# The end of the first batch: four weight chunks, two masks and two column means in new places

## The chip, the cores and the metric

The kernel runs on one core of a Trainium2 chip. The core has five engines that run side by side: TensorE (PE, matrix products), VectorE (DVE), ScalarE (ACT), GpSimd (POOL) and SyncE (SP, which here only issues DMAs). Each takes its own instructions strictly in the order in which the program lists them, and waits where an operand is not ready. The metric is the device time of one execution in microseconds; lower is better.

## The reference

Eight batches of eight heads, 576 positions, 64 channels a head. Attention keeps the 32 largest scores of each row; what comes out is mixed by a two-dimensional Fourier transform whose real part is added to it, normalised, and put through a two-layer network.

```python
scores = scale * np.matmul(q, k.transpose(0, 1, 3, 2))
kth = np.partition(scores, -top_k, axis=-1)[..., -top_k:-top_k + 1]
scores = np.where(scores >= kth, scores, -1000000000.0)
attn = np.exp(scores - scores.max(-1)); attn = attn / (attn.sum(-1) + 1e-09)
x = matmul(attn, v)                       # -> (8, 576, 512)
mixed = np.real(np.fft.fft(np.fft.fft(x, axis=1), axis=2))
u = x + mixed
un = (u - u.mean(-1)) / np.sqrt(u.var(-1) + 1e-06)
out = u + np.maximum(un @ w_ch1, 0.0) @ w_ch2      # 512 -> 2048 -> 512
```

The weights arrive as 64-bit floating point numbers, which the kernel itself turns into 32-bit ones.

## The kernel before

**Attention tiles.** Two heads make a pair, four pairs a batch. A pair has nine tiles of 128 rows of scores; 36 tiles are a batch, 288 the whole. For tile i, PE computes scores (`scores`, L355), ACT copies them to the tile S, and DVE finds the 32 largest of each row in four rounds: `top_ops` (L428) gives an L446 that finds eight maxima and an L448 that strikes them out, seven operations a tile. `bounds` (L451, POOL) prepares two numbers a row, called nt. `mask` (L466) is an ACT operation (L469) and a POOL subtraction (L472), `expo` (L476) the exponential on ACT (L480). In the first batch `transposes` (L532) turns the result by PE and copies it by ACT; in most later ones `plane` (L487, two ACT copies L493) and a transposing DMA do so. `attend` (L576) multiplies by v on PE, `attended` and `to_tokens` bring the result back to rows and normalise it on DVE (L612, L630, L637).

**Weights.** `weight_steps` (L191) converts 32 chunks of 128 x 512: 16 of w1 and 16 of w2. A chunk is loaded by SP into one of five slots of a tile with the tag hT, the same memory in which the hidden activations are kept later. It takes three ACT operations (L209, L225, L228), one DVE shift (L217) and two POOL joins (L236, L238). One chunk is converted beside each of 32 of the first 34 tiles. `centre` (L1433) then makes the columns of w1 zero-mean: PE computes the means of 512 columns in four products (cm, L1437), ACT copies them (L1451), POOL subtracts them from the weights (L1446).

**The end of a batch.** `fold_pair` (L689) adds and subtracts mirrored rows for a pair's 128 channels; POOL does three pairs, and in the first and last batch DVE does the last pair and everything else (`fold_ops`, L751). `fold_tails` (L741) does the 64 rows left over on POOL. `dft_tokens_both` (L780) is the transform along the sequence on PE (yp, L809), whose results ACT copies out (L834 to L847), and `dft_channels` (L849) that along the channels (mp, L860 and L864). `add_at_once` (L877, L880) adds it to x on DVE; `stats` and `rsqrt` follow on DVE (the last is the tile gi) and POOL (L928 to L933). `channels_first` (L935) turns the rows by PE (tpu) and copies them by ACT (unT, L951), and the hidden products (hp, L1055; hT, L1059) begin.

**What sets the order.** The program is written out step by step, one attention tile a step, in the loop at the end of the kernel. A table `plan` holds further work: `at(step, where, fn)` puts a function at a place of a step, and `run(i, where)` calls those due. In step i the loop calls, in this order, the plane copies of tile i-2, the place "convert" (ACT), expo of tile i-1, a list `fixed` of PE work (with the places "pe1", "pe2" and "pe") between which MLP units are strewn, the top-k of tiles i and i+1 (with "shift" among it), `bounds(i)`, in the first batch `mask(i)`, then what has been put off to the end (`late_now`) and the places "dve", "stats", "pool", "pool2" and "load". The order in which these calls are made is each engine's order. The parts around the change:

```python
start_of = [0] + [34 * n // len(wcs) for n in range(1, len(wcs))]
...
at(
    start_of[n1] + 2 + 8 * c if early else PER_BATCH - 4 + 2 * c, "pe1",
    lambda c=c, early=early: centre(c, early), 3.5,
)
...
at((end - 2 if first else end) + hp, "pool2", lambda b=b, hp=hp: fold_pair(b, nc.gpsimd, hp))
```

The first batch ends with tile 35; its fold, in step 37, stands at the place "dve", behind all top-k operations of that step. The scores of tiles 41 and 42, in step 38, stand ahead of the second half of the means and of the transform.

Of the kernel before, what the change touches and what calls it, by code (L numbers as in the profile page):

```python
# [86 lines left out]
def kernel(  # L87
# [1272 lines left out]
    nc.vector.memset(cc[:, 0:1], -1.0)  # L1360

    warm = small.tile([P, 1], F32, name="warm", tag="rd", bufs=6)
    kn0 = batp.tile([P, NC, 2, D], F32, name="kn0", tag="y")
# [55 lines left out]
    nc.sync.dma_start(out=out_list, in_=rows_d.ap())  # L1419
    start_of = [0] + [34 * n // len(wcs) for n in range(1, len(wcs))]  # L1420
    for n, s0 in enumerate(start_of):
# [11 lines left out]
    def centre(c, early):  # L1433
# [18 lines left out]

        if early:
            at(now[0] + 1, "convert", copy)
        else:
            copy()
        for dt in range(NDT):
# [5 lines left out]
    for c in range(DF // DM):  # L1463

        early = c < DF // DM // 2
        at(
            start_of[n1] + 2 + 8 * c if early else PER_BATCH - 4 + 2 * c, "pe1",
            lambda c=c, early=early: centre(c, early), 3.5,
        )
# [13 lines left out]
    for b in range(B):  # L1483
# [4 lines left out]
        for hp in range(NPB - 1):  # L1488
            at((end - 2 if first else end) + hp, "pool2", lambda b=b, hp=hp: fold_pair(b, nc.gpsimd, hp))
        quick = first or last  # L1490
# [98 lines left out]
    while i < N + 5 or plan or queue or sums:  # L1589
# [20 lines left out]
        last_scores = []  # L1610
        if PER_BATCH < j < N and j % PER_PAIR == 0 and by_dma(j):
            fixed.append(lambda: 0.0)
# [27 lines left out]
        n_tr = len(fixed)  # L1640
        if done is not None:
            fixed.append(lambda: transposes(done))
# [16 lines left out]
        turn(i - 3)  # L1659
        if by_dma(i - 1):  # L1660
            mask(i - 1)
        plane(i - 2, 0)
        plane(i - 2, 1)
        run(i, "convert")
        if short:
            expo(i - 1)
        for n, fn in enumerate(fixed):
            cost += fn()
            if n == n_mask:
# [5 lines left out]
                out_next.clear()  # L1675
            if n == min(n_tr, len(fixed) - 1) and PER_BATCH <= i - 1 < N:
                expo(i - 1)
# [26 lines left out]
        first, second = top_ops(i, (2, 3)), top_ops(i + 1, (0, 1))  # L1704
        for n in range(max(len(first), len(second))):
            for ops in (second, first):
                if n < len(ops):
                    ops[n]()
                if ops is first and n == len(first) - 1:
                    run(i, "shift")  # L1710
# [9 lines left out]
        if i < PER_BATCH:  # L1720
            mask(i, lambda: run(i, "join"))
        for fn in late_now:
            fn()
# [44 lines left out]
```

## Time and profile before

| | us |
|---|---|
| median of 3 runs | 1776.76 |
| lowest, highest | 1775.06, 1779.67 |
| profiled execution, its own time | 1780.27 |
| its span, from first to last instruction | 1778.5 |
| PE busy | 1632.1 (92%) |
| DVE busy | 1552.5 (87%) |
| ACT busy | 1278.8 (72%) |
| POOL busy | 906.6 (51%) |

The rows of the profile give a line, an engine, an operation, and `out<-in` by the names of the tiles, with buffer numbers left out. L217 is line 217 of the kernel. "Idle before" is how long the engine had stood still ahead of an instruction, with what ended the wait. Neighbouring instructions on DVE and ACT overlap a little in the trace, so that the step from one start to the next is somewhat less than a duration. The first batch's attention fills the first 225 us, its fold and transform lie between 225 and 250 us.

### The profile page before, as it was taken

What the parts mean: (1) busy time and instruction counts of PE and PEld (TensorE: products, weight loads), DVE (VectorE), ACT (ScalarE), POOL (GpSimd) and SP (SyncE); (2) the same over time, 40 slices, a digit from 0 to 9 for tenths busy, and PEclk for the clock granted to TensorE, in tenths of its full rate; (3) what the DMA queues carried; (4) which work ended last, traced back from release to release, by engine and by line L of the source; (5) the groups of instructions that cost most, each with busy time, mean ns of one, the idle gap of its engine ahead of it and who ended that gap; (6) DMA issues with size and microseconds to landing.
All of it is one profiled execution on the core that took longest, in us unless ns stands there. A gap on an engine that the chain in (4) does not pass through costs nothing.

```text
span 1778.5 us, 26295 instructions
## 1 busy us (share of the span) xinstructions
PE 1632.1 (92%) x7830; PEld 1040.9 (59%) x7830; DVE 1552.5 (87%) x3319; ACT 1278.8 (72%) x3136; POOL 906.6 (51%) x1268
## 2 busy tenths in 40 slices
PE   5666689999898989999999999999999999999998
PEld 3444455464455755566555755576566755577777
DVE  7999989999999999998999999999999999863121
ACT  6888759887787878876888778877978787653200
POOL 4768846655634565354544665356535564333000
PEclk7778799999999999999999999999999999999999
DMA  5333126651457855586557856595558655643151
GB/s 156 115 102 117 32 81 163 185 152 50 119 145 196 222 131 135 136 233 161 135 136 200 212 133 140 152 240 145 152 132 222 182 135 128 172 114 101 36 180 60
DMA packets 492926, 255.28 MB, mean 144 GB/s; under 512 B 364528, under 2 KB 483056, under 8 KB 492784
## 3 DMA queue, kind: packets, MB, share of 16 engines
q1 hardware_dynamic: 489008, 243.80, 52.5%
q0 software_dynamic: 2816, 9.44, 1.6%
q8 instruction: 63, 1.03, 0.2%
q14 instruction: 79, 0.65, 0.1%
q10 hardware_dynamic: 960, 0.36, 0.1%
HBM read 99.79 MB, written 84.74 MB: 104 GB/s over the span
## 4 chain that ended last, share of the span: by engine, by line
PE 48%; DVE 16%; ACT 16%; POOL 14%; issue 5%; DMA 2%; POOLq 0%; SPq 0%; DVEq 0%; ACTq 0%
PE hp L1055 18%; DVE m L446 7%; DVE wk L448 6%; PE o L585 6%; PE cw L1254 5%; POOL wk L472 5%; PE cv L1254 4%; PE sp L422 4%; ACT wk L469 3%; POOL fold L696 3%; PE cp L1120 2%; ACT wk L493 2%; PE cp L1082 2%; ACT S L425 2%; PE sp_t L392 1%
## 5 line engine op out<-in xcount | busy, mean ns | idle before, releaser
L472 POOL TENSOR_TENSOR wk<-S,wk 128x576 f32<-128x576 f32 x288 | 407.6, 1415 | 418.1 <-ACT wk L469 417.2
L446 DVE MAX8 m<-wk 128x8 f32<-128x576 f32 x864 | 617.4, 741 | 0.1
L1055 PE MATMUL hp<-unT,w 128*128 128x256 f32 (+1 forms) x2048 | 529.6, 409 | 6.8 <-ACT hT L1059 6.0
L1055 PEld LDWEIGHTS hp<-unT,w 128*128 128x128 f32 x2048 | 378.0, 191 | 112.0 <-ACT hT L1059 11.4
L448 DVE MATCH_REPLACE8 wk<-m,wk 128x576 f32<-128x576 f32 x576 | 424.8, 737 | 0.0
L469 ACT ACTIVATE wk<-S,nt 128x576 f32<-128x576 f32 x288 | 224.3, 779 | 96.8 <-POOL nt L455 96.3
L493 ACT COPY wk<-S 128x576 uint16<-128x576 uint16 x468 | 290.2, 673 | 0.0
L446 DVE MAX8 m<-S 128x8 f32<-128x576 f32 x288 | 214.5, 745 | 11.6 <-ACT S L396 11.6
L480 ACT ACTIVATE S<-wk,nt 128x576 f32<-128x576 f32 x234 | 185.1, 791 | 46.7 <-POOL wk L472 45.4
L448 DVE MATCH_REPLACE8 wk<-m,S 128x576 f32<-128x576 f32 x288 | 212.5, 738 | 0.0
L1082 PE MATMUL cp<-w,hT 128*128 128x512 f32 x448 | 206.0, 598 | 0.0
L1059 ACT ACTIVATE hT<-hp 128x320 f32<-128x320 f32 (+1 forms) x256 | 104.1, 411 | 140.7 <-PE hp L1055 139.7
L585 PE MATMUL o<-PT,v 128*64 128x256 f32 (+3 forms) x1440 | 196.1, 417 | 5.6 <-DVE wk L448 2.1
L422 PE MATMUL sp<-kT,qT 64*128 64x512 f32 (+1 forms) x528 | 160.1, 668 | 6.7 <-ACT S L414 3.6
L585 PEld LDWEIGHTS o<-PT,v 128*64 128x64 f32 x1440 | 113.2, 154 | 84.1 <-issue 24.8
L425 ACT COPY S<-sp 128x512 f32<-128x512 f32 (+1 forms) x264 | 141.7, 589 | 26.2 <-PE sp L422 25.2
L455 POOL TENSOR_TENSOR nt<-m,cc 128x2 f32<-128x2 f32 x288 | 58.7, 204 | 166.9 <-DVE m L446 160.4
L1254 PE MATMUL cw<-w,hT 128*128 128x256 f32 x512 | 119.7, 383 | 9.1 <-ACT ct L1225 6.2
L1082 PEld LDWEIGHTS cp<-w,hT 128*128 128x128 f32 x448 | 81.3, 193 | 75.1 <-issue 74.7
L392 PEld LDWEIGHTS sp_t<-kt,qT 128*128 128x128 f32 x320 | 51.7, 195 | 111.4 <-issue 73.3
L1254 PEld LDWEIGHTS cw<-w,hT 128*128 128x128 f32 x512 | 94.5, 190 | 27.3 <-ACT ct L1225 8.4
L1254 PE MATMUL cv<-w,hT 128*128 128x256 f32 x432 | 100.4, 383 | 6.6 <-DMA w<-w_parts 2.8
(155 smaller groups left out, 2036.3 us busy)
## 6 DMA issues: line engine op xcount, KB each, us to landing
planes<-wk SPq DMA_DIRECT2D x208, 288.0 KB, 2.7
w<-w_parts SPq DMA_DIRECT2D x94, 512.0 KB, 4.7
space<-in_moe_w_ch_dram SPq DMA_DIRECT2D x32, 512.0 KB, 3.6
nat<-in_q_dram SPq DMA_DIRECT2D x128, 64.0 KB, 2.3
v<-in_v_dram SPq DMA_DIRECT2D x32, 256.0 KB, 3.4
nat<-in_k_dram SPq DMA_DIRECT2D x62, 128.0 KB, 2.8
planes<-wk SPq DMA_DIRECT2D x52, 144.0 KB, 2.7
w_parts<-w_t POOLq DMA_DIRECT2D x8, 512.0 KB, 4.0
```

The lines of the kernel that those rows point to most:

```text
L422: nc.tensor.matmul(sp[r], lhsT=qT[hd, q_cols], rhs=kT[hd, :], start=True, stop=True)
L425: nc.scalar.copy(out=s_t[r, keys], in_=sp[r])
L446: ops.append(lambda src=src, m8=m8: nc.vector.max(out=m8, in_=src))
L448: ops.append(lambda src=src, m8=m8: nc.vector.match_replace(w, m8, src, NEG))
L469: nc.scalar.activation(out=w, in_=Ssb[i], func=AF.Relu, scale=-FAR, bias=Nt[i][:, 1:2])
L472: nc.gpsimd.tensor_tensor(out=w, in0=Ssb[i], in1=w, op=ALU.subtract)
L480: nc.scalar.activation(out=Ssb[i] if by_dma(i) else w, in_=w, func=AF.Exp, bias=Nt.pop(i)[:, 0:1], accum_out=den_t[pair % 3][:, c:c + 1],)
L493: nc.scalar.copy(out=words[:, half, :], in_=src[:, half, :])
L585: nc.tensor.matmul(o[D * e:D * (e + 1), c0:c1], lhsT=vv[:, e, c, :], rhs=pt[:, NF if c == NF else (NF + 1) * e + c, c0:c1], start=(c == 0) ...
L1055: nc.tensor.matmul(hp[:, 0:w], lhsT=w1[:, dt, P * it:P * (it + 1)], rhs=unT[:, dt, 0:w], start=(dt == 0), stop=(dt == NDT - 1),)
L1082: nc.tensor.matmul(cp, lhsT=hT[:, it, P * n:P * (n + 1)], rhs=w2[:, it, :], start=(it == 0), stop=(it == NIT - 1),)
L1254: nc.tensor.matmul(dst, lhsT=h()[a][:, kc, :], rhs=rhs_of(kc), start=start and kc == 0, stop=kc == NK - 1, skip_group_check=True,)
```

## The change

Names by the new code: step 37 is `FOLD_STEP`.

- Of the 32 weight chunks, the last four (the last 512 rows of w2) are no longer converted beside a tile. Their twelve ACT operations stand in step 37 ahead of that step's other ACT work, their four shifts on DVE directly behind the fold, their eight joins on POOL behind it, the last four in step 38. The other 28 are spread over the same 34 steps.
- In step 37 the fold is moved into the top-k list: three operations of tiles 37 and 38 that stood ahead of it now stand behind.
- POOL gets a copy of one column of the fold's last result to an otherwise unused tile, `behind`. Since POOL works in order, what follows there starts when the fold has ended: the subtraction of mask(36), the joins.
- mask(36), moved from the start of step 38; expo(36), plane(36), mask(37), expo(37) and the scores of tiles 41 and 42, which stood ahead of the transform, come behind it.
- The means of w1's first half are computed in steps 21 and 26 instead of 19 and 27, those of the second half in steps 32 and 34 instead of 36 and 38, all of them behind the scores of the step, and their copies by ACT a step later each.
- POOL's folds of the first three pairs stand in steps 31, 33 and 34 instead of 33, 34 and 35.
- In step 35 the transposition of tile 34 goes behind mask(35).

The rest of the program's order is as before.

```diff
+    behind = const.tile([P, 1], F32, name="behind", tag="behind")
...
-    start_of = [0] + [34 * n // len(wcs) for n in range(1, len(wcs))]
+    FOLD_STEP = PER_BATCH + 1
+    LATE = 4
+    n_soon = len(wcs) - LATE
+    start_of = [0] + [34 * n // n_soon for n in range(1, n_soon)]
+    for n in range(n_soon, len(wcs)):
+        at(FOLD_STEP, "convert", lambda n=n: scale_high(n))
+        at(FOLD_STEP, "convert", lambda n=n: rest(n))
+        at(FOLD_STEP, "shift_late", lambda n=n: shift(n))
+        late = n - n_soon
+        for part in range(2):
+            at(
+                FOLD_STEP + late // 2, "join_late" if late == 0 else "pool",
+                lambda n=n, part=part: join(n, part),
+            )
...
-        if early:
-            at(now[0] + 1, "convert", copy)
-        else:
-            copy()
+        at(now[0] + 1, "convert", copy)
...
-            start_of[n1] + 2 + 8 * c if early else PER_BATCH - 4 + 2 * c, "pe1",
+            start_of[n1] + 2 + 5 * c if early else PER_BATCH - 8 + 2 * c, "pe",
...
-            at((end - 2 if first else end) + hp, "pool2", lambda b=b, hp=hp: fold_pair(b, nc.gpsimd, hp))
+            at((end - 4 + (0, 2, 3)[hp] if first else end + hp), "pool2", lambda b=b, hp=hp: fold_pair(b, nc.gpsimd, hp))
...
+        in_lull = FOLD_STEP <= i <= FOLD_STEP + 1
+
+        def postponed():
+            expo(i - 2)
+            plane(i - 2, 0)
+            plane(i - 2, 1)
+            mask(i - 1)
+            expo(i - 1)
+            return 0.0
+
+        if i == FOLD_STEP + 1:
+            fixed.append(lambda: 0.0)
+            last_scores.append(postponed)
+            last_scores.append(lambda: scores(j, 0) + scores(j, 1))
+        elif PER_BATCH < j < N and j % PER_PAIR == 0 and by_dma(j):
...
+        held = done if i == PER_BATCH - 1 else None
+        if done is not None and held is None:
             fixed.append(lambda: transposes(done))
...
-        if by_dma(i - 1):
-            mask(i - 1)
-        plane(i - 2, 0)
-        plane(i - 2, 1)
+        if not in_lull:
+            if by_dma(i - 1):
+                mask(i - 1)
+            plane(i - 2, 0)
+            plane(i - 2, 1)
...
+            if i == FOLD_STEP and n == 2:
+                for fn in late_now:
+                    fn()
+                late_now.clear()
+                run(i, "dve")
+                nc.gpsimd.tensor_copy(out=behind, in_=folded[0][:, 1, DM:LF])
+                run(i, "shift_late")
+                mask(i - 1)
+                run(i, "join_late")
             for ops in (second, first):
...
+        if held is not None:
+            transposes(held)
```

More of the change, by code (lines that the diff above doesn't have):

```diff
@@ L1610 @@
         last_scores = []
-        if PER_BATCH < j < N and j % PER_PAIR == 0 and by_dma(j):
+        in_lull = FOLD_STEP <= i <= FOLD_STEP + 1
[11 more added lines that the diff above has]
+        elif PER_BATCH < j < N and j % PER_PAIR == 0 and by_dma(j):
             fixed.append(lambda: 0.0)
@@ L1640 @@
         n_tr = len(fixed)
-        if done is not None:
+        held = done if i == PER_BATCH - 1 else None
+        if done is not None and held is None:
             fixed.append(lambda: transposes(done))
@@ L1675 @@
                 out_next.clear()
-            if n == min(n_tr, len(fixed) - 1) and PER_BATCH <= i - 1 < N:
+            if n == min(n_tr, len(fixed) - 1) and PER_BATCH <= i - 1 < N and not in_lull:
                 expo(i - 1)
```

## The prediction

> **What bounds the kernel now.** I read the page first (VectorE 87% and TensorE 92% busy, so no single engine), then busy time cut into the stages around the end of the first batch, then the chain that ended last, then the timeline of each engine there. Columns of the first fence: stretch in us from the span's start, its length, then busy us and instructions of PE, PEld, DVE, ACT, POOL, the granted clock, the DMA share, GB/s.
>
> ```profile
> 0.00:193.66 193.66, 121.09 (x598) 75.95 (x599) 183.00 (x385) 156.43 (x362) 136.91 (x137) 0.78 0.37 115
> 193.66:225.04 31.38, 22.14 (x122) 13.93 (x125) 31.28 (x66) 20.99 (x54) 24.24 (x34) 0.76 0.11 28
> 225.04:236.08 11.04, 8.55 (x22) 3.42 (x19) 10.48 (x29) 6.52 (x16) 5.61 (x9) 0.70 0.08 27
> 236.08:249.77 13.69, 12.61 (x96) 9.25 (x95) 9.60 (x24) 7.54 (x27) 0.19 (x1) 0.99 0.16 50
> 249.77:284.30 34.53, 30.83 (x123) 19.69 (x123) 34.29 (x77) 22.50 (x53) 24.41 (x40) 1.00 0.57 144
> 284.30:400.00 115.70, 111.76 (x502) 63.03 (x503) 115.67 (x244) 100.19 (x255) 68.27 (x88) 0.97 0.65 172
> ```
>
> Up to 225 us DVE (the top-k of the first batch) is full but for the start of the program. From 236 to 250 it has 4.1 us of idle, and POOL does nothing. After 250 DVE is full again and PE nearly. So DVE time taken out before 236, and DVE idle filled up to 250, is what can be won. The chain there (start, us, what):
>
> ```profile
> 193.66 1.29 POOL w L236
> ...
> 231.81 5.70 PE cm L1437 x8
> 237.51 5.44 PE yp L809 x56
> ...
> 243.41 0.71 PE mp L860 x4
> 244.12 0.88 PE mp L864 x4
> 245.02 2.74 DVE x L880 x8
> ```
>
> From 193.66 to 225 the chain runs through POOL, ACT and PE of the last tiles, with DVE level beside it; from 228 on it is PE: scores, the two last column means (cm), then the transform (yp, mp), whose result DVE waits for.
>
> **Step A, four shifts leave the DVE-bound stretch.** Total and spread of all 32 (the second row's columns are stretch, length, DVE busy):
>
> ```profile
> L217 DVE TENSOR_SCALAR w<-w x32: 396/704/1474, 22.9 to 203.8; 128x512 int32<-128x512 int32 x32
> 10.00:204.00 194.00, 23.98 (x32) 0.75 0.35 110
> ```
>
> 23.98/32 = 0.75 us, of which some 0.05 overlaps the next instruction: 0.7 each, 4 x 0.7 = 2.8 us earlier (bounds: 4 x 0.35 = 1.4 and 4 x 1.4 = 5.6; I take the mean, since the four steps left out lie anywhere). Their ACT work and their POOL joins (1.29 us each) leave the same steps, on engines with room there. The four loads are only issued some steps later on SP; DMA is 11% busy from 193 on. The means of the first half of w1 move by two steps at most, in PE's idle: nothing.
>
> **Step B, when the fold starts.** Three more top-k operations (0.67, 0.67, 0.73) go behind the fold, so DVE is ready 2.8 + 2.1 = 4.9 us sooner. But the fold also needs the last tile's transposed output, and that chain moves less (single rows of the timeline: start, us, what, and in brackets the idle time before and what ended it):
>
> ```profile
> 197.98 1.12 PE L548 MATMUL tpP<-turns,wk 128*128 128x128 f32 x4 [3.24 <-ACT kT L339]
> 209.73 1.12 PE L548 MATMUL tpP<-turns,wk 128*128 128x128 f32 x4 [3.63 <-ACT wk L480]
> 210.99 2.93 PE L585 MATMUL o<-PT,v 128*64 128x128 f32 x20
> 217.96 3.60 PE L1437 MATMUL cm<-w,ones 128*128 128x512 f32 x8
> 222.72 1.31 PE L585 MATMUL o<-PT,v 128*64 128x128 f32 x18 [0.25 <-ACT PT L551]
> 224.49 0.44 PE L626 MATMUL tpx<-turns,xT 128*128 128x128 f32 x2 [0.46 <-ACT xT L599]
> 231.60 5.91 PE L1437 MATMUL cm<-w,ones 128*128 128x512 f32 x8
> ```
>
> The two late cm (3.60 us at full clock, up to 5.91 after a pause) now fall into the pauses of 3.24 and 3.63 us: between -0.4 and 0 us where PE is at its clock, at worst 2.7 + 2.3 us of delay. In return PE is warm for the o groups behind them (1.31 us for 18 against 2.93 for 20), some 1.2 us each, and the last tile's mask no longer waits for another tile's transposition on ACT (0.5 us). Against that, PE then pauses before the last tile and may do its o at the low rate. I take 0.8 us net for this (bounds -2.1 and +2.0), 2.8 + 0.8 = 3.6: the fold starts at 222.1 instead of 225.7, and DVE waits 1.3 us for it.
>
> **Step C, POOL is kept off the fold.** Again single rows; the last two are the same operations in the last batch's fold, where POOL rests:
>
> ```profile
> 225.76 1.12 DVE L685 TENSOR_TENSOR near<-x 128x256 f32<-128x256 f32 x1
> 228.06 1.51 DVE L696 TENSOR_TENSOR fold<-fold 128x256 f32<-128x256 f32 x1
> 231.92 1.51 DVE L696 TENSOR_TENSOR fold<-fold 128x254 f32<-128x254 f32 x1
> 227.82 1.46 POOL L472 TENSOR_TENSOR wk<-S,wk 128x576 f32<-128x576 f32 x1 [0.89 <-ACT wk L469]
> 231.23 1.92 POOL L472 TENSOR_TENSOR wk<-S,wk 128x576 f32<-128x576 f32 x1 [1.61 <-ACT wk L469]
> 1627.32 0.43 DVE L685 TENSOR_TENSOR near<-x 128x256 f32<-128x256 f32 x1
> 1631.84 0.42 DVE L696 TENSOR_TENSOR fold<-fold 128x254 f32<-128x254 f32 x1
> ```
>
> Each stretched DVE operation overlaps a POOL one. With the small copy into behind ahead of the mask's subtract, POOL stands still until the fold has ended: (1.12 - 0.43) + 2 x (1.51 - 0.42) = 2.9 us (bounds 2.0 and 2.9; the third pair's fold on POOL is a step earlier too). Fold ends at 236.1 - 3.6 - 2.9 = 229.6. I call that time E.
>
> **Step D, from E to the additions.** Before:
>
> ```profile
> 236.08 0.75 DVE L446 MAX8 m<-S 128x8 f32<-128x576 f32 x1
> ...
> 245.02 3.44 DVE L880 TENSOR_TENSOR x<-mp,x 128x512 f32<-128x512 f32 x9 [4.04 <-PE mp L864]
> L630 DVE TENSOR_TENSOR x<-tpx,rd x57: 402/424/426, 57.6 to 1626.9; 128x256 f32<-128x256 f32 x57
> ```
>
> DVE now has the four shifts (0.33 us each alone; one probably meets POOL's subtract, +0.6 taken of 0 to 4 x 1.07), the three operations, 2.1, and the seven it had, 4.9: E + 8.9. PE has paused seven us, so yp begins at the low rate. Its last 48 instructions start at about E - 0.9: 48 x 5.44/56 = 4.7 us at full rate, twice that at half. Behind them come a copy of 0.5 and the first mp, 1.6, so the result is there between E + 5.9 and E + 12 or so. The two cm groups of 8 show a slow spell up to 236.4, eight us after PE resumed at 228.4; the pause of 209.7 ended in one of about 6. With 5 to 6 slow us I take E + 8.5, so DVE sets the time: additions at E + 9.0 = 238.6 against 245.0, 6.4 us earlier. They read PSUM, and L630 of that kind never stretches beside POOL, so additions, statistics and gi keep their 8.0 us. The gain is 2.8 + 0.8 + 2.9 - 0.1 = 6.4.
>
> On the pause, the rows above show the low rate lasting up to 8 us. The Trainium skill, "TensorE: Matmul & The Clock Gate", Part 1, says that the clock falls to half after an idle window of about 3.4 us and comes back after one busy window as long. By that rule yp would lose 1.7 us, mp would come at E + 7.6, and the sum would not change; the trace's slow spells are longer than the rule's.
>
> The shifts stretch up to 1.47 us against 0.40. The Trainium skill, "SBUF — State Buffer", Who interferes with whom, says such an operation and a GpSimd one exclude each other for a whole instruction; if all four met one, DVE would be ready at E + 12.6 and the gain would be 2.8. The L217 row agrees with such waits.
>
> **Step E, POOL and ACT behind the fold.** What an exponential, a mask and a plane take on ACT (all but the last overlap the next operation by 0.1):
>
> ```profile
> 243.64 0.79 ACT L480 ACTIVATE S<-wk,nt 128x576 f32<-128x576 f32 x1
> 244.40 0.79 ACT L469 ACTIVATE wk<-S,nt 128x576 f32<-128x576 f32 x1
> 245.06 1.25 ACT L493 COPY wk<-S 128x576 uint16<-128x576 uint16 x2
> ```
>
> Twelve conversions of 0.57 us fill ACT from 221 to 228, ahead of the y copies and beside the fold. Eight joins, 10.3 us, stand ahead of the reciprocal root. POOL's second subtract waits for ACT's second mask, which follows the y copies (E + 6.8), an exponential, 0.9, a plane, 1.1, and 0.7 for itself: E + 9.5. With subtract and four joins (1.4 + 0.2 + 5.1) POOL is free at E + 16.2; gi is ready at E + 17. Hidden by 0.8 us; each us more delays POOL's masks. ACT then has an exponential, 0.9, score copies, 1.4, a mask, 0.7, a plane, 1.1, all ahead of the unT copies: the hidden products hp start at E + 16.8 = 246.4, only 3.4 us earlier than before:
>
> ```profile
> 249.77 4.57 PE L1055 MATMUL hp<-unT,w 128*128 128x320 f32 x16 [0.61 <-ACT unT L951]
> ...
> 284.32 0.47 PE L329 MATMUL tpq<-turns,qtail 128*128 128x128 f32 x1 [2.40 <-ACT S L396]
> ```
>
> Between 249.77 and 284.3 PE idles 34.53 - 30.83 = 3.7 us. The 3.0 us that PE lags fit into that; I count 0.4 lost. From there the order of work is as before, so the gain is carried to the end: **6.0 us**.
>
> The profiled execution took 1780.27 us (span 1778.5): 1774.3 by this sum. It is 3.5 above the median 1776.76, so for the median 1770.8, 0.34% less. About 0.3%, 5.3 us, is what a measurement can tell here.
>
> **Rivals.**
> *The low clock stays through the transform.* For it: the stage from 225 to 236 had a mean clock of 0.70, and the pause before yp becomes longer. Then mp comes at E + 12.2, additions 3.2 us later, hp at E + 21.5 = 251.1; PE cannot make that up and the gain is about 2.5: 1774.3. Against: yp is 56 instructions without a gap, longer than the spell that warmed PE at 198 to 203.
> *Slower: hT waits for the weights' space.* The chunks are read from the buffer (tag hT) that the first hidden activations write, so ACT's hT, and PE's three banks behind it, wait for the last join. I have it at E + 16.2, with hT due at E + 19; before, the first hT was written 2.5 us after 249.77, at 252.2. The point from which it decides is a last join after 252.2, E + 22.6. If POOL's whole string of subtract and joins, 13.5 us, comes only after ACT's masks at E + 9.5, it ends at E + 23; each us beyond is lost on PE, and with ACT's masks up to 5 us later the time is 1777 to 1782, say 1779.5. For it: four joins stand behind one mask. Against: half of the string needs only the fold.
> *It does not do what it says.* The gain before 250 goes into other idle, since DVE and PE alternate later: 0 to 1 us, 1776. Against: from 249.77 to 400 both are over 95% busy and their order is the same.
>
> **How the numbers follow.** Forecast 0.57 (its own range 1766.5 to 1773; 0.49 of it beyond 0.3%, 0.08 within); low clock 0.20 and no effect 0.08, both within; slower 0.15, of which 0.12 beyond. Faster 0.49, same 0.39, slower 0.12. The range 1766.5 to 1777 leaves out most of the slower case (0.13) and 0.05 of the forecast's better end, a warm PE through step B.
>
> **What would show it.** Shifts gone from four steps and DVE 2.8 us ahead at the last tiles (A); fold start 222 (B); no fold operation over 0.7 us (C); additions at 239 with no DVE idle before (D); last join before gi, hp at 246 (E). Wrong if tpx or mp comes late, if hT waits for POOL, or if PE is still behind at 284.

## The result

The changed kernel takes 1774.78 us (median; 1773.08 to 1778.17) beside 1777.58 us (1774.97 to 1781.54) for the kernel before: a ratio of 0.9984, 95% interval 0.9978 to 0.9989. That is 2.8 us less, where 6.0 were forecast (1770.8 from 1776.76), and half of the 0.3% that the prediction called the bound of a difference. The two profiled executions are not a fair pair: before took 1780.27 us and after 1773.12 us, so their traces differ by 7.1 us; what of that is chance is worked out below.

The page of the changed kernel, its span and busy times; each engine's busy time is within 6 us of what it was:

```profile
span 1771.4 us, 26290 instructions
PE 1630.8 (92%) x7830; PEld 1042.0 (59%) x7830; DVE 1546.9 (87%) x3319; ACT 1278.0 (72%) x3136; POOL 906.5 (51%) x1269
```

Busy time in the prediction's stretches, the same boundaries on the changed kernel (columns as there: stretch, length, PE, PEld, DVE, ACT, POOL, granted clock, DMA share, GB/s):

```profile
193.66:225.04 31.38, 24.76 (x129) 14.33 (x127) 27.26 (x61) 21.18 (x56) 23.13 (x36) 0.83 0.21 62
225.04:236.08 11.04, 7.84 (x42) 6.13 (x38) 10.47 (x34) 9.44 (x26) 3.41 (x3) 0.55 0.00 1
236.08:249.77 13.69, 10.45 (x68) 7.22 (x67) 13.41 (x34) 9.53 (x26) 11.78 (x15) 0.96 0.18 60
249.77:284.30 34.53, 34.53 (x144) 22.34 (x144) 34.53 (x73) 26.52 (x63) 26.99 (x40) 0.97 0.64 169
```

The idle of DVE has changed place. From 236 to 250 it was 4.1 us and is 0.3; from 194 to 225 it was 0.1 and is 4.1. The clock between 225 and 236 fell from 0.70 to 0.55. Behind 250 both DVE and PE are now full.

The timeline of the changed kernel, the rows that answer to the prediction's steps (start, us, engine, line, operation, and in brackets the idle time before and what ended it); PE first, then DVE, POOL and ACT:

```profile
192.97 4.16 PE L1451 MATMUL cm<-w,ones 128*128 128x512 f32 x8
205.06 4.94 PE L1451 MATMUL cm<-w,ones 128*128 128x512 f32 x8
219.07 1.12 PE L548 MATMUL tpP<-turns,wk 128*128 128x128 f32 x4 [2.06 <-ACT qT L337]
220.32 2.92 PE L585 MATMUL o<-PT,v 128*64 128x128 f32 x20
223.71 0.69 PE L626 MATMUL tpx<-turns,xT 128*128 128x128 f32 x2 [0.46 <-ACT xT L599]
238.98 1.03 PE L864 MATMUL mp<-fd,y 128*128 128x256 f32 x4
248.26 6.27 PE L1055 MATMUL hp<-unT,w 128*128 128x320 f32 x16 [2.76 <-ACT unT L951]
223.80 0.18 DVE L612 RECIPROCAL rd<-rd 128x4 f32<-128x4 f32 x1 [3.52 <-ACT rd L611]
224.44 0.42 DVE L630 TENSOR_TENSOR x<-tpx,rd 128x256 f32<-128x256 f32 x1 [0.47 <-PE tpx L626]
224.90 0.43 DVE L685 TENSOR_TENSOR near<-x 128x256 f32<-128x256 f32 x1
226.57 1.61 DVE L696 TENSOR_TENSOR fold<-fold 128x256 f32<-128x256 f32 x4
229.43 0.42 DVE L696 TENSOR_TENSOR fold<-fold 128x254 f32<-128x254 f32 x1
232.52 1.43 DVE L217 TENSOR_SCALAR w<-w 128x512 int32<-128x512 int32 x4
240.73 3.32 DVE L880 TENSOR_TENSOR x<-mp,x 128x512 f32<-128x512 f32 x9
232.67 1.32 POOL L1738 COPY behind<-near 128x1 f32<-128x1 f32 x1 [9.55 <-DVE near L762]
252.47 0.44 ACT L1059 ACTIVATE hT<-hp 128x320 f32<-128x320 f32 x1 [4.26 <-POOL t L928]
```

Read against the prediction: the fold starts at 224.90, not at 222.1, since DVE waits for the last tile (3.52 and 0.47 us), whose o takes 2.92 us where before it took 1.31 behind the means. The fold takes 7.7 us, with no stretched operation. (The two POOL rows that the prediction shows beside the old fold are mask(36) and mask(37); they stood at the start of steps 37 and 38, so mask(36) was moved from step 37, not from step 38.) The additions start at 240.73 with no idle before them. The first hidden products come at 248.26, 1.5 us sooner than before, but take 6.27 us for sixteen where they took 4.57, so the ninth is no earlier than it was. The row of hT names POOL's L928 as what ended its wait; but in all fourteen traces the first hT starts 0.03 to 0.10 us behind the end of the eighth hidden product, so it is PE that it waits for.

### The profile page after: what moved, and what is told of

It reads as the page before. It is cut to its first block, busy times and chain, and to the rows that moved or that the text cites. A ratio compares the mean times of both kernels' runs of the same rounds, so it can differ in the third digit from the quotient of the medians.

```text
span 1771.4 us, 26290 instructions
## 1 busy us (share of the span) xinstructions
PE 1630.8 (92%) x7830; PEld 1042.0 (59%) x7830; DVE 1546.9 (87%) x3319; ACT 1278.0 (72%) x3136; POOL 906.5 (51%) x1269
## 4 chain that ended last, share of the span: by engine, by line
PE 53%; ACT 16%; DVE 11%; POOL 11%; issue 5%; DMA 3%; SPq 1%; POOLq 0%; DVEq 0%; ACTq 0%
PE hp L1055 19%; PE o L585 7%; DVE m L446 5%; PE cw L1254 5%; DVE wk L448 4%; POOL wk L472 4%; PE sp L422 4%; PE cv L1254 4%; ACT wk L469 3%; PE cp L1082 3%; POOL fold L696 3%; PE cp L1120 2%; ACT wk L493 2%; ACT S L425 2%; PE sp_t L392 2%
```

## The experiments

Each run had the kernel before as its neighbour on the same chip, and the ratio is to that. Names of runs stand in bold. Searches (MAX8 on DVE) are counted from the first of the program; the one that the expectations call the 160th is the 161st by this count.

**again** is the changed kernel without an edit, **before_again** the kernel before.

> The changed kernel once more, for a second trace and as the measure of the other runs on this chip. Clock theory: the same times as in the first trace up to 300 us within 0.3 us (fold starting near 224.9, first hidden product near 248.3, DVE 4.2 us ahead of before), because PE's low rate there follows from its pauses. What happens after 500 us (a loss of 2.3 us at 562, where PE waited for a transfer and came back at the low rate) is by that theory a matter of where the pause falls and may be absent here. Rival, that the loss at 562 belongs to the change: it comes again. Ratio to before 0.998 to 0.9985.

> The kernel before once more, for a second trace of the first 220 us. Theory that DVE's shifts are slowed by chance, where one meets POOL: the time at which the 149th maximum starts differs from the first trace's 218.2 by one to three us, with the same operations slow or quick, and the step from there to the 161st, 37.6 us, is the same within 0.5.

The changed kernel again: 1778.3 us, ratio 0.9989 (0.9979 to 1.0). The kernel before, one execution: 1778.86 us. So the gain is 2 to 3 us and no more. Neither trace repeats the first one as closely as was expected: up to 300 us the changed kernel's second trace is off by 1.4 us at the fold and 1.7 at the 149th search, not 0.3, and the step from the 149th to the 161st search in the kernel before is 1.2 us shorter, not within 0.5. The loss at 562 us was absent the second time. These two traces show what chance does to a single one. Times from one search to another, in us, worked out from the traces' starts; the columns are the numbers of the searches:

```
run            1-149  149-161  401-451  451-501  501-521  581-601  601-621  1101-end
before         207.3   37.6     64.2     65.9     28.0     31.2     25.0     267.8
before_again   205.1   36.4     66.7     66.0     28.2     28.7     25.0     269.4
after          204.5   36.1     66.4     65.9     27.3     28.7     24.1     267.7
again          206.1   35.7     64.3     67.3     27.7     28.7     24.4     269.4
```

The 149th search is near the end of the last tile of the first batch, the 161st near the first hidden products. The stretch 1-149 varies by some 2 us within either kernel. At 562 us PE comes back from a pause at full rate or not (the same sixteen products, of before and of after):

```profile
562.16 3.69 PE L1254 MATMUL cv<-w,hT 128*128 128x256 f32 x16 [2.79 <-DMA w<-w_parts]
```

```profile
558.22 5.38 PE L1254 MATMUL cv<-w,hT 128*128 128x256 f32 x16 [3.37 <-ACT S L396]
```

Its 1.7 us are most of what differs in the column 401-451. The kernel before also lost 2.5 us in 581-601 in its first trace, but not in its second. So of the 7.1 us between the first traces some 3 are chance of this kind (2.8 up to the 149th search, as step A below shows, 2.2 the other way in 401-451, 2.5 in 581-601). What both traces of a kernel share is smaller: 149-161, 37.0 to 35.9 in the mean; and 501-521 and 601-621, together 1.3 us less.

**warm_tile**: is it PE's clock that makes the last tile late?

```diff
+    def warmers(n):
+        wm = bank([P, DM], "warm_ps")
+        for _ in range(n):
+            nc.tensor.matmul(wm, lhsT=ident, rhs=w1[:, 0, 0:DM], start=True, stop=True)
+        return 0.0
+
+    at(PER_BATCH, "pe", lambda: warmers(2))
```

> Two products whose result is not used (128x512 each, about 1.8 us at full rate) fill PE's pause of 2.06 us ahead of the last tile's transposition. Clock theory: the transposition takes 0.6 instead of 1.12 us, the o group some 1.75 instead of 2.92, tpx 0.44 instead of 0.69, so the fold starts near 223.0 instead of 224.9, and DVE is 1.9 us further ahead from there on; the time falls by 1 to 2 us against the changed kernel. Queue theory (ACT's order of copies sets the last tile's chain): fold within 0.3 us of 224.9. If two products do not warm PE, the rates will say so.

It took 1773.86 us, ratio 0.9964 (0.9951 to 0.9977). Its timeline, PE (the added products that nothing uses, then the last tile):

```profile
220.79 1.88 PE L1485 MATMUL warm_ps<-w,turns 128*128 128x512 f32 x4
223.02 0.66 PE L548 MATMUL tpP<-turns,wk 128*128 128x128 f32 x4 [0.35 <-ACT qT L337]
...
224.35 1.31 PE L585 MATMUL o<-PT,v 128*64 128x128 f32 x18 [0.20 <-ACT PT L551]
```

The transposition takes 0.66 us, not 1.12, and o 1.31, not 2.92. The fold starts 7.8 us behind the 149th search, where in the five traces of the change without these products it is 9.2 to 9.6: work that computes nothing saves 1.4 to 1.8 us there. That much of the late fold the low rate is shown to cause, not all of it: DVE still waits 2.0 us for the last tile at the full rate, where it waits 3.2 to 3.6 in the change. The time falls by 4.4 us against **again** on the same chip, more than the 1 to 2 expected; where the rest lies was not found.

**no_behind**: is the one-column copy what keeps POOL off the fold?

```diff
-                nc.gpsimd.tensor_copy(out=behind, in_=folded[0][:, 1, DM:LF])
```

> The small copy into behind is left out, so POOL's subtract of the mask for tile 36 may start beside the fold. ACT has its twelve conversions ahead of that mask, which ended at 233.1, after the fold's end at 232.5. Theory that the copy keeps POOL off the fold: a fold operation stretches to 1.5 us again and the fold ends 1 us later. Rival, that the conversions on ACT alone already do it: fold unchanged at 7.6 us, and POOL's subtract starts about 1.1 us earlier, since the copy itself took 1.32 us. Time within 0.5 us of the changed kernel.

It took 1779.0 us, ratio 0.9987 (0.9975 to 0.9998), as the change does, and the fold again takes 7.70 us. POOL's subtraction of mask(36) waited for ACT instead of the copy, and starts 0.8 us sooner behind the fold's end:

```profile
236.66 2.06 POOL L472 TENSOR_TENSOR wk<-S,wk 128x576 f32<-128x576 f32 x1 [10.02 <-ACT wk L469]
```

So the order on ACT (the twelve conversions ahead of the mask) is enough here, and the copy is not needed. (late0 and lull_only below have no conversions there; whether they need the copy was not tried.) The subtraction takes 2.06 us where it meets the shifts; in the changed kernel it was the copy of one column that met them, and took 1.32 us.

**warm_hp** and **unT_first**: what makes the first hidden products late?

```diff
+    def hook(b, t):
+        if b == 0 and t == 4:
+            warmers(3)
+        return 0.0
...
-            at(s + (1 if quick else 2), "pe", lambda b=b, t=t: channels_first(b, t), 0.6)
+            at(s + (1 if quick else 2), "pe", lambda b=b, t=t: channels_first(b, t) + hook(b, t), 0.6)
```

> Three products whose result is not used (some 2.6 us) fill PE's pause of 2.76 us between the turned rows and the first hidden products. Clock theory: the first 16 instructions of the hidden products take 4.6 us instead of 6.27, so the ninth starts near 250.5 instead of 252.2 and PE is 1.7 us further ahead at 255; since DVE and POOL are 4.2 us ahead anyway, the end moves by 0 to 1.5 us. Queue theory (hT and unT on ACT set the pace): the ninth starts at most 0.3 us earlier.

It took 1778.88 us, ratio 0.9986 (0.9976 to 0.9996). The products meant for the pause did not fall into it, as their bank came free only with the copies of unT:

```profile
249.62 4.30 PE L1485 MATMUL warm_ps<-w,turns 128*128 128x512 f32 x6 [2.00 <-ACT unT L951]
253.71 4.75 PE L1055 MATMUL hp<-unT,w 128*128 128x320 f32 x16
```

Sixteen hidden products take 4.75 us behind them, but start later than without. It shows that a PE kept busy makes them faster, and tells nothing of what that is worth. The other run shortens the pause, by putting a mask and two planes behind the copies of unT on ACT:

```diff
+            mask(FOLD_STEP + 1)
+            plane(FOLD_STEP, 0)
+            plane(FOLD_STEP, 1)
...
-        if not in_lull:
+        if not in_lull and i != FOLD_STEP + 2:
```

> On ACT the copies of the turned rows (unT) are put ahead of the mask of tile 38 and the planes of tile 37, 2 us of work that stood before them. Queue theory: the copies then start when PE has turned the rows, some 1.8 us earlier, and the first hidden products start 1.2 to 1.8 us earlier relative to the fold's end. Clock theory adds that PE's pause before them falls from 2.76 to about 1.2 us, so that they need not run at the low rate (4.6 instead of 6.27 us for 16); then the ninth starts 2 to 3.5 us earlier. The mask of tile 38 comes before POOL is free for it (reciprocal root ends 4 us later), so DVE and POOL lose nothing. End: 0.5 to 2 us less than the changed kernel.

```profile
246.63 4.57 PE L1055 MATMUL hp<-unT,w 128*128 128x320 f32 x16 [0.97 <-ACT unT L951]
```

The pause is 0.97 us and the products run at the full rate. The ninth stands 33.3 us behind the 149th search against 36.8 and 36.4. The time is 1775.41 us, ratio 0.9977 (0.9965 to 0.999): about 1 us better than the change, whose interval it meets. The 161st search stands 36.11 us behind the 149th, in the change 36.10, and the 97th hidden product stands 70.53 us behind the 149th search against 70.54: the 3.5 us go into slack that PE has there.

**cm01_back**, **cm01_again**, **late0**, **cm_all_back** and **lull_only** take parts of the change out, the means' new places and the late chunks. Where the means of the first half stand follows from `start_of`, which depends on `LATE`: with `LATE = 4` the edit below puts them at steps 19 and 27, as in the kernel before; in the two runs with `LATE = 0` they stand two steps sooner than the expectations say, at 19 and 24 in late0 and at 17 and 25 in lull_only (in its trace at 109.5 and 155.7 us, in before at 121.6 and 166.3).

```diff
-            start_of[n1] + 2 + 5 * c if early else PER_BATCH - 8 + 2 * c, "pe",
+            start_of[n1] + 8 * c if early else PER_BATCH - 8 + 2 * c, "pe1" if early else "pe",
```

> The changed kernel with the means of w1's first half where they stood before the change (steps 19 and 27, ahead of the score work). In four traces of the new order DVE waits 0.6 to 1.4 us for ACT's L209, 0 to 0.8 for a copy of scores and 0.6 for POOL between 140 and 175 us; before had one wait of 0.6. Theory that these waits come from the four products that now stand between the scores and the transposition: they go but for about 0.6, and everything behind is 0.7 to 2.2 us earlier, so 1 to 2 us less than the changed kernel (ratio to before 0.9975 to 0.9983). Rival, that they come from the denser conversions (28 chunks over the same steps, with shifts meeting POOL): the waits stay, ratio as before, 0.9985.

> The means of w1's first half are back at steps 19 and 27 and behind the transpositions, as in the kernel before; all else of the change stays. It is the same program as the run with the first-half means moved back, measured a second time on its own account. Theory (the 1772.35 us of that run was the means' place): the ratio to the kernel before comes out at 0.9944 to 0.9971 again, about 1771 to 1774 us beside 1779. Rival (it was chance, the shifts and POOL having met seldom in those executions): the ratio is that of the change, 0.9978 to 0.9989, about 1775 to 1777 us. In the trace, whichever holds, the fold starts 7.9 to 9.5 us behind the 149th search and takes 7.7 us.

The same program twice: 1772.35 us, ratio 0.9957 (0.9944 to 0.9971), and 1773.6 us, ratio 0.9967 (0.9955 to 0.9979). Both are better than the change, whose interval the second just touches, and the first by more than the 1 to 2 us expected; the second lies where the first had put it, so it was not chance. The waits of DVE for copies of scores and for POOL did go (0.6 to 1.4 us in the six traces of the new order, none in these two). Its waits for the conversions, which were to go too but for some 0.6 us, did not; the row, from the waits of DVE up to 220 us, has the total, the number and the longest in us, first for the first of these two runs and then for the kernel before:

```profile
DVE w L217 <- ACT w L209: 2.6, 3, 1.5
```

```profile
DVE w L217 <- ACT w L209: 0.6, 1, 0.6
```

So the reason given for that run held for one part of the waits alone and does not account for the 3 to 5 us gained over the change; what causes the waits for the conversions stays open (28 chunks over the same steps stand farther apart than 32, not denser). Next, no chunk late, all 32 beside tiles again:

```diff
-    LATE = 4
+    LATE = 0
```

> All 32 chunks converted beside tiles as before, the rest of the change kept (fold inside the top-k list, masks behind it, means sooner). Theory that the four shifts leave a DVE-bound stretch for one with idle: DVE reaches the last tile's end 2.5 to 3 us later than in the changed kernel, and at the additions it has 1.4 us less to do, which it had no use for; the time is 1.5 to 3 us more than the changed kernel, about that of before. Rival, that DVE waits at the fold anyway (3.2 to 3.6 us in all traces of the changed kernel), so that the moved shifts bought only wait: the fold starts as late as in the changed kernel, relative to the start of the last tiles, and the time is within 1 us of it.

It took 1775.15 us, ratio 0.9977 (0.9967 to 0.9987): with the means in their new places the late chunks gain nothing, as the rival had it. Its fold starts 8.9 us behind the 149th search, with a wait of 3.1 us for the last tile. Then all four means where they were, with the late chunks:

```diff
-        at(now[0] + 1, "convert", copy)
+        if early:
+            at(now[0] + 1, "convert", copy)
+        else:
+            copy()
...
-            start_of[n1] + 2 + 5 * c if early else PER_BATCH - 8 + 2 * c, "pe",
+            start_of[n1] + 8 * c if early else PER_BATCH - 4 + 2 * c, "pe1",
```

> All four means of w1's columns are back where the kernel before has them (the second half at steps 36 and 38); the late chunks, the masks behind the fold and the postponed exponentials stay. Theory (the second half's early means took away the products that kept PE at its full rate for the last tile): the last tile's o is fast again (1.31 us for its longer group, not 2.92), the fold starts 7.6 to 7.9 us behind the 149th search instead of 9.5, and the time is as good as with the first half alone moved back, 1771 to 1775 us. Rival (the early means of the second half pay for that further on, since step 38's eight products of 128x512 would then stand ahead of the first hidden products): the ninth hidden product starts 2 us or more later than 36.8 us behind the 149th search, and the time is 1776 to 1779 us.

It took 1772.68 us, ratio 0.996 (0.9947 to 0.9974), as the theory had it; the fold starts 7.7 us behind the 149th search and the ninth hidden product 34.3, so the rival fell. Its timeline, PE and DVE around the last tile:

```profile
215.85 3.60 PE L1451 MATMUL cm<-w,ones 128*128 128x512 f32 x8
219.29 0.60 PE L548 MATMUL tpP<-turns,wk 128*128 128x128 f32 x4
...
220.62 1.31 PE L585 MATMUL o<-PT,v 128*64 128x128 f32 x18 [0.26 <-ACT PT L551]
...
223.67 3.60 PE L1451 MATMUL cm<-w,ones 128*128 128x512 f32 x8
```

```profile
222.47 0.18 DVE L612 RECIPROCAL rd<-rd 128x4 f32<-128x4 f32 x1 [2.00 <-ACT rd L611]
```

The means in step 36 are work that PE must do in any case, and stand where the unused products of warm_tile stood: the tile behind them is fast. The last mean, of step 38, is fast too, 3.60 us where it took 5.91, now that PE comes to it without a pause. Finally all means back (the first half's two steps sooner than in the kernel before) and no chunk late. What stays of the change is the fold inside the top-k list with three operations behind it, the masks, exponentials and scores behind the fold, the copy into `behind`, POOL's folds of the first three pairs one or two steps sooner and tile 34's transposition behind mask(35):

> All four means are where the kernel before has them, and no weight chunk is late: all eight are converted beside tiles. What stays of the change is that the masks and exponentials of the next tiles come behind the fold, with the one-column copy and the hidden scores behind them. Theory (with the means in their old places PE is fast for the last tile, so DVE no longer waits there and the four late shifts are worth their 2.8 us): 2 to 3.5 us more than with the late chunks and the old means (ratio 0.996, 1772.7), so a ratio of 0.9975 to 0.998, about 1775 to 1776 us beside 1779.5; the 149th search some 2 us later than the 215.6 to 216.6 of the runs with the old means. Rival (four shifts more cost the stretch before it no more than the waits that their absence leaves, as the runs with moved means suggest): the 149th search at 217 or earlier, and the ratio 0.995 to 0.997, about 1772 to 1774 us; then the masks behind the fold carry all of what the change gains.

It took 1770.44 us, ratio 0.9961 (0.9949 to 0.9973). Its profiled execution was the slowest of its six (1774.73), so the trace shows it at its worst; from the timeline, DVE:

```profile
224.53 0.18 DVE L612 RECIPROCAL rd<-rd 128x4 f32<-128x4 f32 x1 [1.44 <-ACT rd L611]
...
225.38 0.43 DVE L685 TENSOR_TENSOR near<-x 128x256 f32<-128x256 f32 x1
...
227.06 1.61 DVE L696 TENSOR_TENSOR fold<-fold 128x256 f32<-128x256 f32 x4
...
239.87 3.32 DVE L880 TENSOR_TENSOR x<-mp,x 128x512 f32<-128x512 f32 x9
```

In its time the theory, that the late shifts are worth 2.8 us once the means are back, fell (0.9975 to 0.998 was expected), and the rival held. In the trace it is the other way: the 149th search stands at 218.20 us, some 2 us later than in the runs with late chunks, as the theory had it, and not at 217 or earlier. From that search to the additions lull_only then takes 21.7 us, where cm_all_back takes 23.6 and the kernel before 26.9 and 25.7: in these traces, what the late shifts save ahead of the search they cost again behind the fold. Four ratios side by side ("where they were" is two steps sooner for the first half's means in the column on the right, as said above):

| | chunks late | no chunk late |
|---|---|---|
| means moved | 0.9984 (0.9978 to 0.9989), the change; 0.9989, again | 0.9977 (0.9967 to 0.9987) |
| means where they were | 0.9960 (0.9947 to 0.9974) | 0.9961 (0.9949 to 0.9973) |

Within a row the ratios agree. What stays in lull_only gains 0.39%, 7 us; no run takes its parts asunder, so that the masks behind the fold earn it is argued from the fold's 7.7 us and the earlier transform, not shown. The late chunks gain nothing that shows: by the intervals at most some 0.8 us in the upper row and some 3 in the lower (estimates from the four intervals). With the chunks late, the moved means take back 0.24%, 4 us, and the intervals do not meet; without, it is 0.16%, and they do.

**cm01_unT_warm** joins the edits of cm01_back, unT_first and warm_tile.

> Three edits to the changed kernel at once: the first-half means back at steps 19 and 27, the mask and the two copies of planes behind the copies of unT on ACT, and two products of 128x512 whose result nothing uses ahead of the last tile's transposition. Theory (the three losses stand at three places, the DVE-bound stretch, the last tile's chain, the first hidden products, and add up): fold start 7.8 us behind the 149th search, ninth hidden product 33 us or less behind it against 36.8, 160th search 34.5 to 35.3 against 36.1, and 1769 to 1772 us, below each of the three alone (1772.35, 1773.86, 1775.41). Rival (the slack of PE until about 560 us absorbs them, so that only what DVE and the next stage see counts): the 160th search is no earlier than with the first-half means alone (34.46), and the time is that one's, 1772 to 1774 us.

It took 1771.22 us, ratio 0.9957 (0.9942 to 0.9972). In its trace DVE waits 0.34 us for the last tile, the fold starts 6.1 us behind the 149th search, and the 161st search comes 33.45 us behind it, all better than expected; the time is that of lull_only, which has neither the unused products nor the other order of the copies. Both are below the kernel before by 0.4% and below the change by more than 0.2%; lull_only is the simpler of the two.

Where the moved means lose it, from the traces without added products ahead of the last tile (start of the fold; start of the additions, in us from the span's start):

| | fold starts | additions start |
|---|---|---|
| kernel before, 2 traces | 225.8, 223.5 | 245.0, 241.5 |
| means moved, chunks late, 5 traces (after, again, no_behind, warm_hp, unT_first) | 224.9 to 228.4, mean 226.3 | 240.7 to 244.2, mean 242.2 |
| means moved, no chunk late (late0) | 226.4 | 242.2 |
| first half where it was, 2 traces | 224.5, 224.5 | 240.3, 240.6 |
| all means where they were, chunks late | 223.3 | 239.2 |
| all means back, the first half's two steps sooner, no chunk late (lull_only) | 225.4 | 239.9 |

By the means of these the moved first half costs 1.7 us at the additions and the moved second half 1.3 (a single trace stands for the last). That is 3.0 of the 4 us in the times; the rest is within what single traces scatter.

## Why the prediction was right in its direction and wrong in its size

**Step A, "four shifts leave the DVE-bound stretch", -2.8 us: failed.** In the first pair of traces it seems exact: the 149th search is at 215.39 against 218.18 us. But up to that search six programs are one and the same (after, again, no_behind, warm_tile, warm_hp, unT_first; the added products of warm_tile start behind it), and they have it at 215.4 to 219.3, mean 217.3; the kernel before has it at 218.2 and 215.9, mean 217.0, and late0, with no chunk late, at 217.5. The shifts' own work does become less, about as the step had it: the 28 ahead of that search take 19.4 to 22.1 us, mean 20.7, in the ten traces with late chunks, the 32 of the other four 21.7 to 24.3, mean 22.8. (A shift takes 0.40 us or 1.0 and more, depending on whether it meets POOL, so the total spreads by 2 us with the order unchanged.) But in the six traces DVE stands idle 2.2 to 3.9 us up to there, and 1.44 and 1.55 in the kernel before: it waits longer for ACT and POOL, of which the step said only that there is room. With the first half's means back the same search is at 215.6 to 216.6 (four traces, mean 216.0), 1.3 us sooner in the mean; so "the means of the first half of w1 move ... in PE's idle: nothing" seems to have hidden a cost, though the ranges of the single traces overlap. And what the shifts save ahead of the fold, they take again behind it, 1.43 us. The prediction counted that in step D and set it against DVE's idle ahead of the additions. In lull_only, without the late shifts, no such idle is left and the additions come at E + 6.8; in late0, where mp is later, 1.27 us of it are. No single trace could settle this; the two pairs of times, late0 beside the change and lull_only beside cm_all_back, leave the late chunks no gain that shows.

**Step B, fold at 222.1: failed, by the possibility it named.** "PE then pauses before the last tile and may do its o at the low rate" is what happens, in every trace of the change; 0.8 us of gain had been taken out of -2.1 to +2.0, and it is a loss of 1.4 to 1.8 by warm_tile. The moved means of the second half take 4.16 and 4.94 us in the pauses of 3.24 and 3.63 that were to hold them at -0.4 to 0, as the clock is low behind each pause (0.50 granted from 190.69 to 194.10 and from 204.34 to 207.76 us). The rows of before spoke for the loss: its o behind a pause of 3.63 us takes 2.93, its o behind the means 1.31, and the change takes those means away. With A it makes the fold start 1.7 us later than before in the means of the traces, not 3.6 earlier.

**Step C, -2.9 us: right in kind, 2.1 to 2.7 in size.** The fold takes 7.70 us in every changed kernel, 10.40 and 9.82 in the two traces of before: in the second of these two of the three operations are stretched to 1.5 us and `near` only to 0.55, so the third was chance in the trace that gave the price. The copy, to which the step ascribed it, is not needed where ACT has the conversions ahead of the mask (no_behind).

**Step D, E + 9.0: 8.2.** E, where the fold's last operation gives way to the next, is 232.5 us here. All four shifts are free of POOL (1.43 us together, 0.6 had been added for one that meets it). PE runs yp at the low rate until 235.06 us (granted clock 0.55 between 225 and 236) and the rest of it at the full one. The first mp ends at 240.0, E + 7.5 where 8.5 had been taken, 0.7 us ahead of the additions, so DVE sets the time, as the step had it. The rival of the low clock fell: its condition, the low rate through the whole transform, did not come. That the median, 1774.8, lies where that rival had put it (1774.3) is chance. The Trainium skill, "TensorE: Matmul & The Clock Gate", Part 1, has the clock fall after one idle window of about 3.4 us that runs freely, whatever the kernel does. The trace agrees, in that the granted clock changes only at the ends of windows of 3.41 us; but such a window need not be empty. The one from 214.59 to 218.00 us, with 1.39 us of PE work in it, was enough to make the last tile slow, and the pause of 2.06 us lies across its end (columns as in the stretches above):

```profile
214.59:218.00 3.41, 1.39 (x9) 0.72 (x7) 3.41 (x8) 2.37 (x7) 2.10 (x5) 1.00 0.12 29
218.00:221.41 3.41, 2.34 (x13) 1.77 (x15) 2.28 (x6) 1.88 (x6) 3.02 (x8) 0.50 0.28 62
```

**Step E: POOL right, hp's rate missed.** The last join ends at 248.4 us, E + 15.9 for 16.2; POOL is free 0.5 us before gi; hT does not wait for the chunks' space, so the slower rival fell. The hidden products come 1.9 us later than forecast because the fold ends 2.9 us later; behind E they come 1.1 us sooner than the step had, E + 15.7 for 16.8. What no step had priced is their low rate behind a pause of 2.76 us, 1.7 us for sixteen. That the 3.7 us of PE's slack absorb such a lag was right: unT_first removes it and gains about 1 us, less than its interval.

**The sum.** Steps A and B were to give 3.6 and gave -1.7; C and D were to give 2.8 and gave some 2.8 to 3. That leaves 1.1 at the additions (242.2 against 243.3), and the later stretches named above, which no step had, add 1.3: 2.4 of the 2.8 measured. So the steps together gave 1.1 us of 6.4; that the time still fell within the range is owed to these later stretches and to the range's width. Without the moved means the same parts give 7 us, more than the forecast: in lull_only 3.4 at the additions (4.6 when counted from the 149th search, which is late in its trace), 1.3 or so later; the other 2 its one trace, 4.3 us above its median, does not show, and where they lie stays open.

## What to carry over

Moving work off a full engine gained nothing here, where it went to another place at which that engine was nearly full; price the moved instructions at both ends. And see that an edit that takes one part out does not move another with it, as `LATE = 0` moved the means. Work that stands in front of a critical chain can keep PE at its rate: before moving it, look at what the chain's products take behind work and behind a pause, in the same trace. Where a kernel's traces scatter by some us from chance meetings of two engines, take the price of such a meeting from several traces, and settle a part of a change by leaving it out on the chip, in all combinations.

## What the runs showed of the hardware that was not expected

The same pause can leave PE at either rate: 2.76 us ahead of the hidden products, 6.27 us for sixteen in the change, and in warm_tile

```profile
251.38 4.58 PE L1055 MATMUL hp<-unT,w 128*128 128x320 f32 x16 [2.75 <-ACT unT L951]
```

The record of the granted clock tells the two apart. In every trace it changes only at the ends of windows of 3.41 us, whose ends fall at another place of the program in each trace (2.6 us behind the 149th search in after, 2.1 in again, 3.0 in no_behind). In the change the whole pause lies within one such window, which holds 0.65 us of PE work, and the next window has the clock at 0.50 (columns as in the stretches above):

```profile
245.31:248.72 3.41, 0.65 (x6) 0.44 (x4) 3.17 (x11) 2.90 (x6) 2.98 (x3) 1.00 0.14 43
248.72:252.13 3.41, 3.41 (x8) 2.19 (x7) 3.41 (x8) 0.00 (x0) 2.33 (x12) 0.50 1.02 330
```

In warm_tile the end of a window cuts the pause in two, each of the two windows holds more work, and the clock stays at 1.00 (the products after them run at the full rate, as the row above shows):

```profile
246.23:249.64 3.41, 2.40 (x18) 1.45 (x14) 3.27 (x9) 3.41 (x9) 3.33 (x4) 1.00 0.02 5
249.64:253.05 3.41, 1.67 (x6) 1.25 (x7) 3.27 (x8) 1.69 (x4) 2.56 (x6) 1.00 0.50 166
```

In the fourteen traces, from 100 us on, the clock fell behind every full-rate window with less than 1.47 us of PE work, behind none with more than 1.95, and between the two behind some. So a pause shorter than a window slows PE or not by where it falls, and that is part of the chance between two traces of one program.

POOL's copy of one column took 1.32 us behind DVE's first shift, and 0.19 us where DVE had a search instead (late0):

```profile
234.14 0.19 POOL L1738 COPY behind<-near 128x1 f32<-128x1 f32 x1 [8.87 <-DVE near L762]
```

The shift and POOL's instruction take turns whole. The Trainium skill, "SBUF — State Buffer", Who interferes with whom, says so of such operations and that the one issued first goes through; the four shifts at 0.36 us each with POOL's copy beside them at 1.32 agree with it.
